# Attention, SoLU FFN and ReLU6 FFN on one core: a list scheduler gets a modelled transfer queue, a smaller cushion and another table of moves

## The chip, the cores and the metric

The kernel runs on one NeuronCore of a Trainium2 chip. The metric is the device time of one execution in microseconds (us); of several runs the median is taken.

## What is computed

Three stages in a row, all in float32 (the reference is cut to them):

```
# q, k, v: 4 x 8 heads x 576 positions x 64;  s: 4 x 8 x 576
scores = q @ k.T / sqrt(D);  cum = cumsum(max(s, 0))
scores = where(causal, -1e9, scores + min(-(cum_i - cum_j), 0))
x = softmax(scores) @ v                     # 2304 tokens x 512
h = x @ w_in                                # 512 -> 1024
solu = h * softmax(h);  x = (layernorm(solu) * g_ln) @ w_out
h = x @ w_in2                               # 512 -> 2048
g = h * clip(h + 3, 0, 6) / 6;  out = g @ w_out2
```

## The kernel before

Every float32 operand of a matmul is split into a high and a low part of reduced width, and a product is made of three matmuls (high by high, high by low, low by high). The splits are what ACT and DVE do most: ACT casts the high part, DVE subtracts it to get the low one.

**Attention** goes by pairs of heads: q and k are transposed on TensorE (L679, L639 for the first heads), stacked, the scores are made (L794, L830), the exponent is taken on ACT (L751), the rows are scaled on POOL (L846, L864), transposed (L898) and multiplied by v (L925). **The SoLU FFN** works on 18 tiles of 128 tokens: first product L1030, exponent L1047 and square L1067 on ACT, transposes L1099, second product L1120. Its tiles run in between the heads. **The ReLU6 FFN** starts when the last tile of the SoLU FFN has its second product: three groups `bi` of 768 tokens and eight slices `k` of the hidden width make 24 units. A unit does seven products of blocks on TensorE instead of eight (L1370, six matmuls each): it needs the seven forms of x (`xb`, cast at L1309 from the loaded tile `xr`), the seven forms of the weights of slice k (`ws`, cast at L480, low part at L484), and it collects its results through ACT copies out of PSUM (`c`, L1383), DVE sums (L1389), the clip on ACT (L1396) and the product on DVE (L1399). Each result `g` is stored to DRAM (`g_d`, L1404), in the last slices from POOL's queue. The second product (L1547) loads it back (`r`, L1504), splits it into forms (`fa`, `fs`, L1524) and multiplies it by the forms of the second weights (`W`, either loaded whole at L1464 or loaded into `stage` at L1453 and split at L1457 and L1460).

**What sets the order.** Nothing is issued while the program above is walked. Each operation is recorded by `plan.add(eng, us, fn, reads, writes, ...)` as one of 4138 entries with its engine, an assumed duration, and what it depends on. `Plan.emit` (L99 to L187) then plays them through: each engine takes, of the entries whose inputs are there, the one of lowest `rank`; PSUM banks and buffers are given out on the way. The entries are then issued in the order in which they started in this play, and each engine runs its own entries strictly in that order. So the assumed durations, the assumed landing times of transfers (`lag`), a cushion per engine (`plan.spare`, set at L1219 and added to every DVE and ACT entry recorded after it) and the table `MOVED` (L45), which adds a number to the rank of a range of entries, decide which instruction of an engine stands ahead of which, and nothing else. An instruction whose input is late holds up all that stand behind it on its engine.

```
for a, b, eng, places in MOVED:
    for i in range(a, b):
        if eng in (None, self.ops[i][0]):
            self.rank[i] += places
...
ready_at[j] = max(ready_at[j], end + lag + hop if done else start)
```

Of the kernel before, what the change touches and what calls it, by code (L numbers as in the profile page):

```python
# [42 lines left out]
X_RAW = 2  # L43

MOVED = (  # L45
    (2969, 3058, None, 37), (1088, 1095, None, -26), (42, 207, "ACT", -571), (89, 289, None, 22), (701, 705, None, -5000), (1603, 1616, None, -575),
    (3219, 3238, None, -136), (1310, 1376, "PE", -5000), (4000, 4010, None, 9), (3187, 3354, None, 10), (2195, 2220, None, -5000), (1728, 1743, None, 80),
    (1680, 1785, None, -19), (3311, 3318, None, 11), (1751, 1784, "DVE", 600), (3833, 3890, None, 20), (3402, 3431, None, -110), (4067, 4090, None, 5000),
    (2726, 2734, None, 7), (2064, 2078, None, 7), (3604, 3653, None, 7), (3738, 3763, None, -890), (3446, 3458, None, -1115), (193, 393, "ACT", -14),
    (99, 112, "ACT", -173),  # L50
# [4 lines left out]
class Plan:  # L55


    def __init__(self):
        self.ops, self.writers, self.users, self.rings, self.born, self.reuse = [], {}, {}, {}, {}, []
        self.takes, self.bank = {}, {}  # L60
        self.stage, self.stages = "", {}
        self.behind, self.rank, self.port = 0, [], []
        self.spare = {}

    def add(self, eng, us, fn, reads=(), writes=(), new=(), lag=0.0, bank=None, after=(), stages=(), port=None):
# [3 lines left out]
        self.port.append(eng == "POOL" if port is None else port)  # L69
        self.rank.append(op + self.behind)  # L70
# [34 lines left out]
    def emit(self):  # L105
# [30 lines left out]
        order, port_free = [], 0.0  # L136
        while len(order) < n:
# [25 lines left out]
            us, lag = self.ops[i][1], self.ops[i][4]  # L163
# [3 lines left out]
            free[e] = end = start + us  # L167
            order.append((start, i))
# [15 lines left out]
        for _, i in sorted(order):  # L184
            self.ops[i][2]()

# [22 lines left out]
def kernel(ctx, tc, q, k, v, s, w_in, w_out, g_ln, w2_in, w2_out, out):  # L209
# [81 lines left out]
    def gate_rows():  # L291
# [37 lines left out]
        for i in range(len(blocks)):  # L329
            plan.add("ACT" if i >= 2 else "SP", 0.45, lambda i=i: load(i), writes=[f"s/{i}"], lag=2.0)  # L330
# [9 lines left out]
        def to_dram():  # L340
            plan.add("POOL", 0.6, lambda: nc.gpsimd.tensor_scalar(neg, first_t["cum"][: 2 * NH].bitcast(F32), -1.0, 1.0, ALU.mult, ALU.mult), reads=["gate/h", "gate/l1"], writes=["neg"])
            for x in range(2):
                r = blocks[x]
                for i, row, src, keys in ((0, 2 * x, lambda r: one[:NH], ["one"]), (1, 2 * x + 1, lambda r: one[:NH], ["one"]), (1, 2 * x, lambda r: first_t["cum"][r].bitcast(F32), ["gate/h", "gate/l1"]), (0, 2 * x + 1, lambda r: neg[r], ["neg"])):
                    plan.add("SP", 0.45, lambda i=i, row=row, src=src, r=r: put(i, row, src(r)), reads=keys, writes=[f"rows/{i}{row}"], lag=4.0)
# [13 lines left out]
    def split64(plan, pool, src, hi, lo, name, key, scale=None, bufs=1, ring="", raws64=2, after=(), hi_dve=False, on_dve=(), on_act=(), behind=None, needs=(), home=()):  # L359
# [44 lines left out]
        def put_lo():  # L404
# [3 lines left out]
            else:  # L408
# [5 lines left out]
                             lag=2.0 if behind is None else 4.0, after=after),  # L414
# [1247 lines left out]
```

## Time and profile before

| | |
|---|---|
| runs shown | 793.2, 796.46, 796.31 us; median 796.31 |
| the profiled execution | 792.05 us, span 790.3 us |
| busy: PE, DVE, ACT, POOL | 769.4 (97%), 598.3 (76%), 476.5 (60%), 233.0 us (29%) |
| mean granted TensorE clock | 0.994 |

Times in the trace are microseconds from the start of the span. The profiled execution took 1.75 us more than its span and 4.26 us less than the median of the runs. "PEclk" is the granted share of TensorE's full clock. A matmul is pipelined, so its own duration in the trace is longer than the distance to the next one; a stretch in which matmuls follow each other without a hole counts as fully busy.

### The profile page before, as it was taken

What the parts mean: (1) busy time and instruction counts of PE and PEld (TensorE: products, weight loads), DVE (VectorE), ACT (ScalarE), POOL (GpSimd) and SP (SyncE); (2) the same over time, 40 slices, a digit from 0 to 9 for tenths busy, and PEclk for the clock granted to TensorE, in tenths of its full rate; (3) what the DMA queues carried; (4) which work ended last, traced back from release to release, by engine and by line L of the source; (5) the groups of instructions that cost most, each with busy time, mean ns of one, the idle gap of its engine ahead of it and who ended that gap; (6) DMA issues with size and microseconds to landing.
All of it is one profiled execution on the core that took longest, in us unless ns stands there. A gap on an engine that the chain in (4) does not pass through costs nothing.

```text
span 790.3 us, 15882 instructions
## 1 busy us (share of the span) xinstructions
PE 769.4 (97%) x5560; PEld 706.1 (89%) x5560; DVE 598.3 (76%) x1381; ACT 476.5 (60%) x1071; POOL 233.0 (29%) x320
## 2 busy tenths in 40 slices
PE   6899999999999999999999999999998999999998
PEld 5667888988889888888999999999998999999998
DVE  5889988688967786838797898889886866666662
ACT  5979887667666666736474665666674444444341
POOL 3676726263533454243110000000131012213122
PEclk9999999999999999999999999999998999999999
DMA  9947688785587757523533544666589644444440
GB/s 208 230 144 186 167 206 219 208 211 162 135 216 181 218 138 187 142 74 114 171 97 108 188 157 177 218 213 216 178 299 377 194 146 127 127 137 130 134 134 28
DMA packets 157616, 136.34 MB, mean 173 GB/s; under 512 B 67616, under 2 KB 135200, under 8 KB 157536
## 3 DMA queue, kind: packets, MB, share of 16 engines
q1 hardware_dynamic: 153600, 122.07, 53.8%
q10 hardware_dynamic: 2400, 8.54, 3.3%
q0 software_dynamic: 1536, 4.72, 1.5%
q8 instruction: 44, 0.72, 0.4%
q14 instruction: 36, 0.29, 0.1%
HBM read 74.67 MB, written 39.39 MB: 144 GB/s over the span
## 4 chain that ended last, share of the span: by engine, by line
PE 84%; DVE 7%; DMA 6%; issue 1%; ACT 1%; POOL 1%; SPq 0%; DVEq 0%; ACTq 0%; POOLq 0%
PE bank L1547 23%; PE bank L1370 17%; PE bank L1030 11%; PE bank L1120 10%; PE bank L925 6%; PE bank L898 6%; PE bank L830 5%; PE bank L794 2%; PE bank L1099 2%; DMA stage<-wt_d 2%; DMA rawi<-in_moe_w_in_dram 2%; PE bank L679 1%; DMA xr<-x_d 1%; DMA r<-g_d 1%; DVE xb L1312 1%
## 5 line engine op out<-in xcount | busy, mean ns | idle before, releaser
L1370 PE MATMUL bank<-xb,ws 128*128 128x384 f32 x1008 | 179.4, 339 | 5.9 <-ACT c L1383 4.7
L1370 PEld LDWEIGHTS bank<-xb,ws 128*128 128x128 f32 x1008 | 177.0, 189 | 7.3 <-ACT c L1383 5.7
L1547 PE MATMUL bank<-W,fs 128*128 128x256 f32 x864 | 105.7, 282 | 0.0
L1547 PEld LDWEIGHTS bank<-W,fs 128*128 128x128 f32 x864 | 104.1, 190 | 0.0
L846 POOL TENSOR_SCALAR y<-y,rsum 128x128 f32<-128x128 f32 (+4 forms) x120 | 73.0, 627 | 91.7 <-DVE rsum L842 56.5
L751 ACT ACTIVATE y<-y,nmax 96x576 f32<-96x576 f32 (+4 forms) x140 | 83.2, 596 | 12.2 <-DVE nmax L739 7.2
L739 DVE CUSTOM_DVE_ANT_0 y<-bank,mask 96x288 f32<-96x288 f32 (+4 forms) x168 | 73.9, 465 | 20.9 <-PE bank L830 16.9
L1120 PE MATMUL bank<-zh,w_out_h 128*128 128x256 f32 x288 | 82.9, 288 | 0.0
L1547 PE MATMUL bank<-W,fa 128*128 128x256 f32 x648 | 81.1, 284 | 0.0
L1120 PE MATMUL bank<-zh,w_out_l 128*128 128x256 f32 x288 | 81.0, 281 | 0.0
L1120 PE MATMUL bank<-zl,w_out_h 128*128 128x256 f32 x288 | 80.9, 281 | 0.0
L1547 PEld LDWEIGHTS bank<-W,fa 128*128 128x128 f32 x648 | 79.5, 192 | 0.0
L1404 POOL DMA_DIRECT2D g_d<-g x24 | 13.2, 552 | 195.5 <-DVE g L1399 195.4
L1030 PE MATMUL bank<-w_in_h,xh 128*128 128x512 f32 x144 | 61.1, 424 | 2.0 <-DVE nmax L739 2.0
L1030 PE MATMUL bank<-w_in_h,xl 128*128 128x512 f32 x144 | 56.9, 395 | 0.0
L830 PE MATMUL bank<-stack 128*96 128x288 f32 (+4 forms) x288 | 56.7, 317 | 0.1
L1030 PE MATMUL bank<-w_in_l,xh 128*128 128x512 f32 x144 | 56.7, 394 | 0.0
L1120 PEld LDWEIGHTS bank<-zh,w_out_h 128*128 128x128 f32 x288 | 54.2, 188 | 1.9 <-issue 0.7
L1383 ACT COPY c<-bank 128x384 f32<-128x384 f32 x72 | 34.1, 479 | 34.6 <-PE bank L1370 32.8
L1120 PEld LDWEIGHTS bank<-zh,w_out_l 128*128 128x128 f32 x288 | 54.3, 188 | 0.4
L1120 PEld LDWEIGHTS bank<-zl,w_out_h 128*128 128x128 f32 x288 | 54.2, 188 | 0.0
L898 PE MATMUL bank<-ident,y 128*128 128x128 f32 (+2 forms) x420 | 51.8, 259 | 0.5 <-POOL y L864 0.3
(275 smaller groups left out, 1572.7 us busy)
## 6 DMA issues: line engine op xcount, KB each, us to landing
r<-g_d SPq DMA_DIRECT2D x36, 512.0 KB
g_d<-g SPq DMA_DIRECT2D x72, 192.0 KB
rawo<-in_moe_w_out_dram SPq DMA_DIRECT2D x16, 512.0 KB
rawi<-in_moe_w_in_dram SPq DMA_DIRECT2D x16, 512.0 KB
x_d<-x2s SPq DMA_DIRECT2D x36, 128.0 KB
xr<-x_d SPq DMA_DIRECT2D x6, 768.0 KB
g_d<-g POOLq DMA_DIRECT2D x24, 192.0 KB, 4.8
W<-wp_d SPq DMA_DIRECT2D x6, 768.0 KB
```

Source lines behind the costliest of these rows:

```text
L739: nc.vector.tensor_tensor_reduce(out=ys[h, t][:n, c0:c1], in0=bank(key)[:n, : c1 - c0], in1=mask[:n, 480 + n - w + c0 : 480 + n - w + c1], ...
L751: nc.scalar.activation(out=y[:n], in_=y[:n], func=AF.Exp, bias=nmax[:n, h, t : t + 1], scale=-1.0, accum_out=sums[:n, h, t : t + 1])
L794: nc.tensor.matmul(bank(keys[j])[:n, : c1 - c0], lhsT=a, rhs=b, start=(m == 0), stop=(m == 3))
L830: nc.tensor.matmul(bank(key)[:n, : c1 - c0], lhsT=ss[:, 2 - 2 * m, ST[t] : w], rhs=ss[:, 3 - 2 * m, c0:c1], start=(m == 0), stop=(m == 1))
L846: nc.gpsimd.tensor_scalar(ys[h, t][:n], ys[h, t][:n], rsum[:n, h, t : t + 1], 1.0, ALU.mult, ALU.mult)
L898: nc.tensor.transpose(bank(key)[: SZ[jj], c : c + SZ[t]], ys[h, t][: SZ[t], ST[jj] : ST[jj] + SZ[jj]], ident[: SZ[t], : SZ[t]])
L925: nc.tensor.matmul(bank(key)[j * D : (j + 1) * D, lo - c0 : c1 - c0], lhsT=vs[v_key(p, a)][:n, jj, j, :], rhs=pts[pt_key(2 * p + j, a)][:n ...
L1030: nc.tensor.matmul(bank(key), lhsT=xs[i][m // 2][:, kk, :], rhs=(w_in_l if m == 1 else w_in_h)[:, kk, f * 512 : (f + 1) * 512], start=(kk ...
L1120: nc.tensor.matmul(bank(key)[:, : 2 * P], lhsT=w_out_at(w, kk)[:, m * P : (m + 1) * P], rhs=z[:, kk, :], start=(kk == 0 and i == 0), stop= ...
L1370: nc.tensor.matmul(bank(key)[:, :W], lhsT=T[f"ws{k}"][:, WS_OF[op], a, kc * P : (kc + 1) * P], rhs=x_form(bi, op)[:, b, kc, :], start=(fir ...
L1383: nc.scalar.copy(T[to], bank(key)[:, :W])
L1547: nc.tensor.matmul(bank(b_key)[:, : 2 * P], lhsT=T[name][:, y, k, :], rhs=T[f"W{i}_{q}"][:, k - k0, w, :], start=first and k == 0 and y == ...
```

## The change

Three edits, all in the planning; the operations, their engines, their dependencies and the number of instructions of each engine stay as they are.

1. A transfer no longer lands a fixed `lag` after its issue. It is given a size (`dma=moved(rows, size)`), and all transfers pass through one queue, one after the other.
2. The cushion for DVE and ACT goes from 0.03 and 0.05 us to 0.01 and 0.02 us.
3. The 25 ranges of `MOVED` are replaced by 26 others.

```diff
+DMA_START, DMA_END = 1.3, 0.3

 MOVED = (
-    (2969, 3058, None, 37), (1088, 1095, None, -26), (42, 207, "ACT", -571), (89, 289, None, 22), (701, 705, None, -5000), (1603, 1616, None, -575),
...
+    (2125, 2234, None, 171), (3467, 3487, "DVE", -24), (1445, 1447, None, 136), (4113, 4128, None, -127), (1025, 1031, None, -31), (2338, 2339, None, -64),
...
+            if self.dma[i]:
+                dma_free = max(end + DMA_START, dma_free) + self.dma[i]
+                landed = dma_free + DMA_END - end
...
-                ready_at[j] = max(ready_at[j], end + lag + hop if done else start)
+                ready_at[j] = max(ready_at[j], end + landed + hop if done else start)
...
+def moved(rows, size):
+    return rows * (0.0087 + 0.0000368 * size) * 1.13 / 16
...
-            plan.spare = {"DVE": 0.03, "ACT": 0.05, "POOL": 0}
+            plan.spare = {"DVE": 0.01, "ACT": 0.02, "POOL": 0}
...
-                    "SP", 0.0016 * 2 * P * (k1 - k0), load, reads=[f"wt{k}/{WT_PART[i]}" for k in range(k0, k1)], writes=[f"{key}s", *first], new=ring, after=["stage"], lag=2.5),
+                    "SP", 0.0016 * 2 * P * (k1 - k0), load, reads=[f"wt{k}/{WT_PART[i]}" for k in range(k0, k1)], writes=[f"{key}s", *first], new=ring, after=["stage"], dma=moved(128, 1024 * (k1 - k0))),
...
```

All other `lag=` become `dma=` in the same way. Below line 330 the lines of the changed kernel are 9 higher.

What it does to the order: every engine's instructions are the same, 316 of 1486 PE entries, 178 of 1057 on DVE, 99 of 874 on ACT, 12 of 447 on SP and 3 of 274 on POOL stand more than five places from where they stood. Three places:

ACT, end of the first product of the ReLU6 FFN, before (`c_7` is a result of slice 7 copied out of PSUM, `g_6_01` a clipped result of slice 6, `W_2_7317` the high part of a piece of the second weights, cast out of the loaded `stage`):

```order
761 L1383 COPY c_6_7271<-bank_102 128x384
762 L1396 ACTIVATE g_6_11_7290<-c_6_7271 128x384
763 L1396 ACTIVATE g_6_10_7294<-bank_102 128x384
764 L1383 COPY c_7_7304<-bank_97 128x384
765 L1457 CAST W_2_7317<-stage 128x2x256
766 L1383 COPY c_7_7325<-bank_97 128x384
767 L1396 ACTIVATE g_6_01_7328<-c_6_7244 128x384
768 L1396 ACTIVATE g_7_00_7338<-c_7_7259 128x384
769 L1396 ACTIVATE g_7_11_7342<-c_7_7325 128x384
```

and now:

```order
763 L1392 COPY c_6_7275<-bank_96 128x384
764 L1405 ACTIVATE g_6_11_7288<-c_6_7275 128x384
765 L1405 ACTIVATE g_6_10_7297<-bank_96 128x384
766 L1405 ACTIVATE g_6_01_7309<-c_6_7242 128x384
767 L1405 ACTIVATE g_7_00_7319<-c_7_7264 128x384
768 L1392 COPY c_7_7322<-bank_101 128x384
769 L1392 COPY c_7_7347<-bank_101 128x384
770 L1466 CAST W_2_7349<-stage 128x2x256
771 L1405 ACTIVATE g_7_11_7365<-c_7_7347 128x384
```

The cast out of `stage` stood ahead of the last `c_7` copy and stands behind it now; two clips, `g_6_01` and `g_7_00`, have come ahead of both copies.

PE at the same place, before (L1370 is the first product of the FFN, L1547 the second):

```order
2517 L1370 MATMUL bank_97<-xb_5_5683,ws_6903 128x384 x6
2518 L1370 MATMUL bank_100<-xb_4_5663,ws_6903 128x384 x6
2519 L1370 MATMUL bank_97<-xb_3_5758,ws_6903 128x384 x6
2520 L1370 MATMUL bank_100<-xb_6_5643,ws_6903 128x384 x6
2521 L1547 MATMUL bank_101<-W_0_6948,fa_0_0_7164 128x256 x6
2522 L1547 MATMUL bank_101<-W_1_6981,fa_0_0_7164 128x256 x6
2523 L1547 MATMUL bank_101<-W_2_7089,fa_0_0_7164 128x256 x4
```

and now:

```order
2517 L1379 MATMUL bank_97<-xb_4_5683,ws_6888 128x384 x6
2518 L1556 MATMUL bank_98<-W_0_6967,fa_0_0_7121 128x256 x6
2519 L1379 MATMUL bank_101<-xb_5_5695,ws_6888 128x384 x6
2520 L1556 MATMUL bank_98<-W_1_6982,fa_0_0_7121 128x256 x6
2521 L1556 MATMUL bank_98<-W_2_7062,fa_0_0_7121 128x256 x4
2522 L1379 MATMUL bank_101<-xb_3_5745,ws_6888 128x384 x6
2523 L1379 MATMUL bank_97<-xb_6_5666,ws_6888 128x384 x6
```

Sixteen matmuls of the second product have come in between the last four groups of the first.

ACT some 35 us into the ReLU6 FFN, where x of the second group of tokens is split, before (`xb_6` is cast out of `xr_1`, the second of its two loaded halves; `c_0` and `c_1` are results of the first and second slice copied out of PSUM):

```order
561 L1396 ACTIVATE g_1_10_5620<-bank_102 128x384
562 L1309 CAST xb_0_5630<-xr_0_5589 128x768
563 L1396 ACTIVATE g_1_01_5640<-c_1_5546 128x384
564 L1309 CAST xb_6_5643<-xr_1_5600 128x768
565 L1396 ACTIVATE g_0_00_5652<-c_0_5591 128x384
566 L1383 COPY c_0_5654<-bank_95 128x384
567 L1309 CAST xb_4_5663<-xr_0_5589 128x768
568 L1309 CAST xb_1_5666<-xr_1_5600 128x768
569 L1383 COPY c_1_5674<-bank_99 128x384
```

and now:

```order
562 L1405 ACTIVATE g_1_10_5620<-bank_96 128x384
563 L1405 ACTIVATE g_1_01_5632<-c_1_5547 128x384
564 L1405 ACTIVATE g_0_00_5640<-c_0_5590 128x384
565 L1318 CAST xb_0_5643<-xr_0_5599 128x768
566 L1392 COPY c_0_5653<-bank_102 128x384
567 L1392 COPY c_1_5657<-bank_99 128x384
568 L1318 CAST xb_6_5666<-xr_1_5608 128x768
569 L1318 CAST xb_1_5675<-xr_1_5608 128x768
```

The cast of `xb_6` stood ahead of `g_0_00` and the copies `c_0` and `c_1` and stands behind all three now.

Four more moves are spoken of below. On ACT, at the start of the ReLU6 FFN, the casts of the first slice's weights (`ws`, L480) stood behind the two exponents of the last SoLU tile and stand ahead of them now; on DVE their low parts (L484) stand four places earlier, ahead of that tile's own steps (L1051 to L1062). On PE the products of the first group with the last slice of weights stand three to four places earlier. On ACT the cast of the first form of the second product (`fa_0_0`, L1524, out of the loaded `r`) stands four places earlier, now ahead of a `c_7` copy that PE waits for, and SP issues that load two places earlier. In the attention stage, 20 to 48 us, PE has the scores of a later block (13 places earlier) and six transposes ahead of the first matmuls of the SoLU FFN (L1030), on DVE some steps of the row maximum (L739) come 16 to 24 places earlier, and on POOL six scalings of rows (L864) stand ahead of the low part of the first SoLU tile (`xl`, L1016).

## Rows read from the trace of the kernel before

**Rows 1.** The page: busy us (share of the span) and instructions of each engine.

```profile
PE 769.4 (97%) x5560; PEld 706.1 (89%) x5560; DVE 598.3 (76%) x1381; ACT 476.5 (60%) x1071; POOL 233.0 (29%) x320
```

**Rows 2.** Waits of PE: awaited line, us in total, times, longest.

```profile
PE bank L639 <- DMA rawq<-in_q_dram: 6.0, 2, 5.4
PE bank L1370 <- ACT c L1383: 4.7, 2, 3.2
PE bank L1030 <- DVE nmax L739: 2.0, 1, 2.0
PE bank L1370 <- DVE ws L484: 1.0, 1, 1.0
```

**Rows 3.** Windows: length, busy us by engine, PEclk, DMA share, GB/s.

```profile
20.00:40.00 20.00, 17.57 (x148) 12.47 (x150) 16.12 (x65) 18.39 (x53) 12.53 (x17) 1.00 0.92 227
40.00:60.00 20.00, 18.04 (x130) 12.93 (x127) 16.37 (x46) 16.02 (x38) 16.51 (x18) 0.91 0.51 150
44.40:47.90 3.50, 3.50 (x13) 2.11 (x12) 2.69 (x8) 2.67 (x7) 3.50 (x5) 0.51 0.50 162
...
100.00:380.00 280.00, 279.87 (x2078) 241.64 (x2077) 212.48 (x651) 185.44 (x484) 119.44 (x187) 1.00 0.64 170
...
400.00:420.00 20.00, 18.85 (x147) 18.39 (x146) 18.30 (x37) 15.63 (x32) 1.52 (x3) 1.00 0.26 80
460.00:580.00 120.00, 120.00 (x690) 120.00 (x689) 102.83 (x206) 76.97 (x162) 4.11 (x8) 1.00 0.58 197
580.00:600.00 20.00, 18.60 (x106) 17.96 (x104) 13.70 (x25) 10.71 (x21) 6.40 (x12) 1.00 1.01 369
600.80:607.70 6.90, 5.88 (x21) 5.88 (x22) 4.75 (x8) 4.24 (x8) 2.15 (x4) 0.51 0.97 365
620.00:780.00 160.00, 160.00 (x1346) 160.00 (x1345) 104.60 (x97) 65.16 (x88) 34.96 (x14) 1.00 0.42 124
```

**Rows 4.** Timeline around 402 us: start, us, engine, line, operation.

```profile
401.99 0.61 ACT L480 CAST ws<-ai 128x512 fp32r<-128x512 f32 x1
...
402.65 0.44 PE L1370 MATMUL bank<-xb,ws 128*128 128x384 f32 x1
...
403.36 1.02 DVE L484 TENSOR_TENSOR ws<-ai,ws 128x512 fp32r<-128x512 f32 x2
...
404.10 0.44 PE L1370 MATMUL bank<-xb,ws 128*128 128x384 f32 x1 [1.00 <-DVE ws L484]
```

**Rows 5.** Timeline around 445 us.

```profile
444.77 0.83 ACT L1309 CAST xb<-xr 128x768 fp32r<-128x768 f32 x1 [2.08 <-DMA xr<-x_d]
...
445.50 0.52 ACT L1396 ACTIVATE g<-c 128x384 f32<-128x384 f32 x1
...
445.93 0.46 ACT L1383 COPY c<-bank 128x384 f32<-128x384 f32 x1
...
446.44 0.44 PE L1370 MATMUL bank<-xb,ws 128*128 128x384 f32 x1 [1.56 <-ACT c L1383]
```

**Rows 6.** Timeline around 601 us.

```profile
600.77 0.62 ACT L1457 CAST W<-stage 128x512 fp32r<-128x512 f32 x1 [4.55 <-DMA stage<-wt_d]
601.30 0.47 ACT L1383 COPY c<-bank 128x384 f32<-128x384 f32 x1
...
601.82 0.69 PE L1370 MATMUL bank<-xb,ws 128*128 128x384 f32 x1 [3.19 <-ACT c L1383]
```

**Rows 7.** Timeline around 584 us, ACT, and DVE before it.

```profile
568.11 0.68 DVE L484 TENSOR_TENSOR ws<-ai,ws 128x512 fp32r<-128x512 f32 x1
...
584.01 1.05 ACT L1524 CAST fa<-r 128x1024 fp32r<-128x1024 f32 x1 [1.86 <-DMA r<-g_d]
```

**Rows 8.** Chain of waits, two links: start, us from issue to landing.

```profile
577.20 6.79 DMA r<-g_d
...
591.34 9.40 DMA stage<-wt_d
```

**Rows 9.** Transfers issued from 589 to 592.4 us: number, KB, median us to landing.

```profile
g_d<-g POOLq DMA_DIRECT2D x3, 192.0 KB, 6.5
```

More of the change, by code (lines that the diff above doesn't have):

```diff
@@ L329, in gate_rows @@
         for i in range(len(blocks)):
-            plan.add("ACT" if i >= 2 else "SP", 0.45, lambda i=i: load(i), writes=[f"s/{i}"], lag=2.0)
+            plan.add("ACT" if i >= 2 else "SP", 0.45, lambda i=i: load(i), writes=[f"s/{i}"], dma=moved(32, 2304))
         plan.add("DVE", 0.55, lambda: nc.vector.memset(one, 1.0), writes=["one"])
@@ L592, in load_qk @@
                 new, room = ([("x", 2, "x0")], []) if name == "q" else ([], ["x0/raw"])
-            plan.add("SP", 1.1, lambda name=name, src=src: rows(name, src), reads=room, writes=[key], new=new, lag=4.0)
+            plan.add("SP", 1.1, lambda name=name, src=src: rows(name, src), reads=room, writes=[key], new=new, dma=2 * moved(576, 256))
     def v_key(p, a):
@@ L611, in load_v @@
         for j in range(2):
-            plan.add("SP", 0.5 + 0.5 * a, lambda j=j: values(j), writes=[f"{key}/{j}"], new=[("V", 2, key)] if j == 0 else [], lag=3.0, after=[begun(p)])
+            plan.add("SP", 0.5 + 0.5 * a, lambda j=j: values(j), writes=[f"{key}/{j}"], new=[("V", 2, key)] if j == 0 else [], dma=moved(576 if a else 256, 256), after=[begun(p)])
     def first_home(p, name):
@@ L1208 @@
     to_dram()
-    plan.add("SP", 0.5, lambda: nc.sync.dma_start(out=g_sb, in_=g_ln.rearrange("(c p) -> p c", p=P)), writes=["g"], lag=2.0, after=["HL0k/h0"])
+    plan.add("SP", 0.5, lambda: nc.sync.dma_start(out=g_sb, in_=g_ln.rearrange("(c p) -> p c", p=P)), writes=["g"], dma=moved(1024, 4), after=["HL0k/h0"])
     for b, share in enumerate(SHARES):
@@ L1468, in weights @@
                 r.append(lambda both=both, key=key, k0=k0, k1=k1, number=number: plan.add(
-                    "SP", 0.0032 * 2 * P * (k1 - k0), both, reads=[f"wt{k}/{WT_PART[i]}" for k in range(k0, k1)], writes=[f"{key}/h", f"{key}/l"], new=[(f"rm{number}", 1, key)], lag=2.5))
+                    "SP", 0.0032 * 2 * P * (k1 - k0), both, reads=[f"wt{k}/{WT_PART[i]}" for k in range(k0, k1)], writes=[f"{key}/h", f"{key}/l"], new=[(f"rm{number}", 1, key)], dma=moved(128, 2048 * (k1 - k0))))
                 continue
@@ L1504, in go @@
                 nc.sync.dma_start(out=T[key(x)], in_=g_d[bi, h, o, :, :, t * P : (t + 1) * P])
-            return lambda: plan.add("SP", 1.6, go, reads=[f"gd{bi}_{h}{o}/{k}" for k in range(NK)] + (["forms"] if mine[x] == 4 else []), writes=[key(x)], new=raw_new(x), lag=3.5)
+            return lambda: plan.add("SP", 1.6, go, reads=[f"gd{bi}_{h}{o}/{k}" for k in range(NK)] + (["forms"] if mine[x] == 4 else []), writes=[key(x)], new=raw_new(x), dma=moved(1024, 512))
         def total(to, a, b, op):
```

36 lines of the change are left out of this document (17 added, 19 removed), and 3 rows, old and new, of the table MOVED.

## The prediction

> **What bounds the kernel now.** I read the busy times first: PE is busy 769.4 us, 97% of the span [rows 1]. The number of matmuls stays, so the change can only win, or lose, what PE loses in waits and in half clock. Of the 790.3 us of the span 20.9 are not PE's (790.3 - 769.4). The waits of PE name most of them [rows 2]: 6.0 us for the first q, before any of the moves acts; 4.7 for ACT's copies of L1383, in two waits; 2.0 at L1030; 1.0 for a weight form at L484. The rest is shorter waits, the start and the last stores.
>
> Then the windows [rows 3], to place these waits and the clock. From 100 to 380 us PE is busy for 279.87 of 280 us, and from 460 to 580 and 620 to 780 all the time: there the change can win nothing. What can be won lies in 20 to 60 us (2.43 and 1.96 us not busy), 400 to 420 (1.15), around 445 and 580 to 608. In two stretches the granted clock is half, 1.2 GHz instead of 2.4: 44.4 to 47.9 (mean 0.51), after PE stood 2.0 us for L1030 [rows 2], and 600.8 to 607.7 (0.51), after it stood 3.19 us [rows 6]. Work that takes 3.5 us at this level takes 1.8 at the other, 6.9 takes 3.5. The waits of 1.00 and 1.56 us [rows 4, 5] were not followed by half clock.
>
> **The change part by part.** The new durations and landings of the play are no times of the chip; they matter only through the order that comes out. So I went through each place in which PE waits, and through the moved entries for places in which it might.
>
> *Start of the ReLU6 FFN (402 us).* PE's first L1370 matmul starts at 402.65, the next at 404.10, for one low part of the weights that DVE gives from 403.36 on, because ACT's cast ran from 401.99 to 402.60, behind two exponents [rows 4]. Back to back they would be 0.17 us apart (unit of six 1.04 us), so 1.3 us are lost here, and 0.3 before the first. In the new order ACT's cast stands ahead of both exponents and DVE's low part ahead of the tile's steps. I let it end near 402.6 and leave 0.2 us: **-1.4**. What gets later are the exponents of the last SoLU tile; its tokens are needed by the third group only, some tens of us later, which hides them.
>
> *xb_6 (445 us).* ACT's cast at 444.77 waited 2.08 us for the loaded half of x; behind it stood a clip and the copy c_0 (445.93), and for this copy PE stood 1.56 us [rows 5]. Now the clip and the copy stand ahead of the cast. They wait for PE alone, so the copy ends over 1 us before PE comes (its distance in the new order): **-1.6**, bounds 0 and -1.7. Late next is xb_6 itself: PE needs it some units of 1.04 us later, and later copies arrive within 0.2 to 0.4 us of their need, which I count below.
>
> *The end of the first product (598 to 608 us).* The cast out of stage started at 600.77 after 4.55 us of waiting, the last c_7 copy at 601.30, PE at 601.82 after 3.19 us [rows 6]. The load behind it took 9.40 us from issue to landing [rows 8]; the play assumed 2.5. Now the copy stands ahead of the cast, and PE has sixteen matmuls of the second product (0.72, 0.72 and 0.48 us) between the last first products. PE's 3.19 us go, and with them, if no other hole of this size opens, the half clock (3.4 us): 6.6. Against it: the two clips that now stand ahead of both copies need buffers freed by stores, which land late here (6.5 us from issue [rows 9]), 0.5 us; the forms of the second product are made only when the last first product is done, and PE is there with less in hand, 0.5 us. **-5.5**, bounds -6.6 and -1 (the hole only gets shorter and the clock falls all the same). The cast of stage is needed first some 4 us after this place, and is there.
>
> *Products with the last slice, three to four places earlier (566 us).* DVE gives the low part of their weights at 568.11 to 568.79 [rows 7]; the products come about 3.5 us sooner, DVE's entry only about 2. **+1.2**, bounds 0 and +2; such a wait was not followed by half clock at 1.56.
>
> *fa_0_0 ahead of a c_7 copy (580 us).* ACT starts this cast at 584.01, as soon as its load lands, after 1.86 us of waiting [rows 7]; the load was issued at 577.20 and took 6.79 us [rows 8]. On SP it now stands two places earlier, and the last result that it loads is stored about 3 us sooner. It then lands near 580.5, and the copy behind it still comes before PE needs it (582.5): 0, bounds 0 and +6.9 (below).
>
> *20 to 60 us.* 4.4 us of holes and 1.7 of half clock. The 2.0 us in front of L1030 is filled by scores and six transposes that now stand there; POOL's six scalings come ahead of xl and make L1030 itself later, and DVE's steps of the row maximum (about 1 us) push the low parts of the next heads, so two short waits grow. DVE, ACT and POOL are each busy 12 to 18 of 20 us here. **-1.5**, bounds +1 (a new hole of 1 us, clock unchanged) and -4.
>
> *All other moves and the smaller cushion.* I found about ten places at which an entry of PE now comes within 0.3 us of its input; each may cost 0 to 0.3: **+1.3** in sum, bounds 0 and +3. On SP only 12 and on POOL 3 entries move over five places; their transfers shift with PE.
>
> Sum: -1.4 - 1.6 - 5.5 - 1.5 + 1.2 + 1.3 = -7.5 us. The profiled execution, 792.05 us (span 790.3 and 1.75 around it), would take 784.5. It stands 4.26 under the median of the runs shown (796.31); carried over to it: 788.8 us. No trace shows what the runs at 796 had in addition; if it hangs on the holes removed here, the gain is larger.
>
> **A rule against it.** The new play lets all transfers through one queue in their order of issue. The trace of the stretch where it matters most does not: the load issued at 591.34 took 9.40 us [rows 8], while three stores of 192 KB that POOL issued between 589 and 592.4 took a median of 6.5 [rows 9]; at least the ones issued after 591.34 were done before it. The Trainium skill, "DMA: Bandwidth & Descriptors", section "Queues, rings and completion order", says that a DMA engine goes round the queues that have work, packet by packet, and that completion is not in order of issue. By that rule the play has SP's loads too early wherever POOL stores, as here; the trace agrees.
>
> **The rivals.** *The load of fa_0_0 comes late.* If SP's load lands as before, at 584.0, since POOL's stores are served beside it, ACT stands at its cast with a c_7 copy behind, which ends near 586 instead of before 582.5. PE then has a hole of 3.5 us, as long as the one of 3.19 that was followed by half clock: 3.5 + 3.4 = 6.9 us back, -0.6 in sum, 795.7. For it: the 6.79 us of this load, and the full DMA engines (share 1.01 [rows 3]). Against it: issue and store come earlier. It decides from 1.5 us of lateness on. Chance 0.14.
>
> *The hole at 598 us moves and the clock still falls.* Clips wait for buffers, copies stand behind them, and two holes of 1 to 2 us follow each other: of 6.6 us only 1 to 1.5 stays won, -7.5 + 4.5 = -3, 793.3. For it: a hole of 2.0 us was followed by half clock at 44.4 [rows 2, 3]. Against: the sixteen matmuls in between. Chance 0.10. That the change does nothing at all can be told from the order to be untrue.
>
> *The small cushion costs PE time in the full windows (slower).* With less slack a planned start meets inputs that are late on the chip, and 316 PE entries stand elsewhere. If each of the some 14 windows from 100 to 380 us lost as much as that from 400 to 420 does now (1.15 us [rows 3]), that is 16 us, -7.5 + 16 = +8.5, 804.8; it decides from 0.54 us per window (7.5 / 14). For it: DVE and ACT are busy 212 and 185 of these 280 us, so a late step is not made up at once. Against: 0.01 to 0.03 us per entry is small beside durations of 0.5, and I found only some ten tight places. Chance 0.14.
>
> **How the numbers follow.** Forecast 0.62, rivals 0.14, 0.10 and 0.14. About 0.5% (4 us) is what a measurement of this kernel can tell from no change. The forecast lies beyond it, below 792.3; the first two rivals lie within it, together 0.24; the third beyond it on the other side. The range goes from 783 (all of 598 to 608 won and the early stage near its bound) to 797, which takes in the first two rivals and leaves out most of the third and the far ends of the forecast.
>
> **What would show it.** PE's wait list: no wait of over 0.5 us for L1383's copies near 445 and 601; 20.00 busy near 402; granted clock full from 580 to 620; no hole near 580. A wait of PE for the last ws7 form near 562 to 566 of about 1 us. I am wrong if the wait list shows a new hole over 2 us from 60 to 400, if ACT waits over 1.5 us for the first r with PE standing behind it, or if half clock remains near 600.

## The result, and the profile after

The changed kernel took 782.81 us (median of four runs, 781.96 to 783.54), before 794.94 (four runs, 793.2 to 796.46). The ratio is 0.9848, 95% interval 0.9819 to 0.9876: 1.5% faster. Four more executions made later, beside eleven of before, gave 782.96 us and 0.9859 (0.9844 to 0.9875). Five single executions of 808 to 2615 us, far from all others of their kernel, are left out of the medians and ratios here and below. The profiled execution of the changed kernel took 783.54 us with a span of 781.7, 8.5 us less than the one of before (792.05). The forecast of 788.8 had the direction right and 6.0 us too little gain; 782.81 lies 0.2 us under the low end of the range, 783.

The page of the changed kernel, busy times, and the slices of PE and its clock:

```profile
PE 766.9 (98%) x5560; PEld 705.5 (90%) x5560; DVE 600.4 (77%) x1381; ACT 476.8 (61%) x1071; POOL 229.0 (29%) x320
...
PE   6999999999999999999999999999999999999998
...
PEclk9999999999999999999999999999999999999999
```

The work of the other engines is as before to within 4 us [rows 1]. PE's busy time fell by 2.5 us: before, some 9.4 us of it lay in the two half-clock stretches (3.50 and 5.88 [rows 3]), and now there is one of 3.4 us. Its waits now (line numbers are 9 higher):

```profile
PE bank L648 <- DMA rawq<-in_q_dram: 5.6, 2, 5.4
PE bank L648 <- DMA rawk<-in_k_dram: 1.2, 1, 1.2
PE bank L934 <- ACT pt4a L911: 0.9, 1, 0.9
PE bank L688 <- DVE HL6q L700: 0.7, 1, 0.7
PE bank L907 <- POOL y L873: 0.7, 2, 0.5
```

The waits for ACT's copies (4.7 us), for L484 (1.0) and in front of L1030 (2.0) of [rows 2] are gone from the list. Four of the five shown lie in the first 46 us; the one in front of L688 is new and stands at 101 us. The windows that answer to [rows 3]:

```profile
20.00:40.00 20.00, 18.31 (x140) 13.30 (x140) 14.68 (x63) 17.48 (x52) 12.13 (x19) 0.91 0.82 208
40.00:60.00 20.00, 19.02 (x147) 14.01 (x148) 17.05 (x53) 16.91 (x40) 16.99 (x18) 1.00 0.70 182
...
100.00:380.00 280.00, 279.30 (x2078) 241.57 (x2076) 213.05 (x656) 184.31 (x483) 118.98 (x186) 1.00 0.65 169
...
400.00:420.00 20.00, 20.00 (x158) 20.00 (x158) 18.06 (x34) 13.37 (x28) 0.86 (x2) 1.00 0.18 56
...
440.00:460.00 20.00, 20.00 (x117) 20.00 (x116) 18.24 (x29) 13.95 (x27) 0.00 (x0) 1.00 0.46 162
460.00:580.00 120.00, 120.00 (x690) 120.00 (x689) 104.84 (x210) 79.78 (x166) 5.64 (x10) 1.00 0.62 205
...
580.00:600.00 20.00, 20.00 (x124) 20.00 (x123) 13.84 (x26) 11.22 (x23) 6.79 (x13) 1.00 1.04 379
600.00:620.00 20.00, 19.65 (x163) 19.24 (x162) 16.98 (x18) 9.48 (x13) 0.77 (x2) 1.00 0.89 316
```

The places at 402 and 445 us are full, from 580 to 620 PE lacks 0.35 us, and all of them run at the full clock. One half-clock stretch is left, of 3.4 us in the first window. The place at 598 us, ACT and PE:

```profile
596.06 0.48 ACT L1392 COPY c<-bank 128x384 f32<-128x384 f32 x1 [1.94 <-PE bank L1379]
596.43 0.63 ACT L1466 CAST W<-stage 128x512 fp32r<-128x512 f32 x1
...
595.86 1.36 PE L1556 MATMUL bank<-W,fa 128*128 128x256 f32 x10
597.06 2.26 PE L1379 MATMUL bank<-xb,ws 128*128 128x384 f32 x12
...
586.78 0.32 SPq L1462 DMA_DIRECT2D stage<-wt_d  x1
```

The copy waits for PE and for nothing else. The cast behind it, for which ACT stood 4.55 us [rows 6], does not wait at all: SP issues its load at 586.8 now, at 591.3 before [rows 8].

One measure serves all runs below: the **late stretch**, from the first matmul of the ReLU6 FFN (402.65 in [rows 4]) to the start of the last matmul, as the timeline of PE shows them. Before it is 402.65 to 786.55, 383.90 us; in the changed kernel 402.90 to 778.14, 375.24 us, 8.66 us less. In these two executions the changed kernel reaches its beginning 0.25 us later than the one of before: the whole difference between them lies in the late stretch.

Start and length are those of each kernel's profiled execution. The ratio is to before's executions taken beside that kernel, so ratios compare better than medians do.

| kernel | median us | ratio to before, 95% | start of late stretch | late stretch |
|---|---|---|---|---|
| before | 794.94 | 1 | 402.65 | 383.90 |
| changed | 782.81 | 0.9848 (0.9819 to 0.9876) | 402.90 | 375.24 |
| before again | 793.88 | 0.9998 (0.9979 to 1.0016) | 403.95 | 383.99 |
| last cast behind last copy (C) | 790.4 | 0.9954 (0.9938 to 0.997) | 405.04 | 381.06 |
| 402 and 445 us (A, B) | 789.79 | 0.995 (0.9932 to 0.9968) | 404.90 | 381.17 |
| A, B, C | 788.33 | 0.9921 (0.9901 to 0.9941) | 405.05 | 377.90 |
| A, B, C, cast further back | 789.4 | 0.9956 (0.9933 to 0.9979) | 404.11 | 378.95 |
| five moves | 790.6 | 0.9961 (0.994 to 0.9983) | 405.65 | 379.40 |
| seven moves | 786.44 | 0.9891 (0.9868 to 0.9914) | 404.55 | 376.59 |
| change's order up to 318 us | 791.87 | 0.9981 (0.9963 to 0.9998) | 400.70 | 383.93 |
| change's order from 318 us | 785.23 | 0.9906 (0.9885 to 0.9928) | 403.38 | 375.25 |
| queue, small cushion, old moves | 795.3 | 1.0017 (1.0 to 1.0035) | 412.05 | 378.67 |
| queue alone | 794.42 | 0.9998 (0.9975 to 1.0022) | 410.94 | 377.51 |
| new moves alone | 811.01 | 1.023 (1.0201 to 1.0259) | 421.58 | 384.74 |
| changed, old cushion | 789.57 | 0.9936 (0.9913 to 0.9958) | 405.39 | 377.61 |
| changed, two more moves | 781.61 | 0.9844 (0.9826 to 0.9862) | 400.03 | 376.07 |
| changed again | 782.96 | 0.9859 (0.9844 to 0.9875) | 401.98 | 375.62 |

Two columns of this table say more than the pair of profiled executions did. The late stretch hardly differs between executions of one order: 383.90, 383.99 and 383.93 us where the order from 318 us on is that of before, 375.24, 375.25 and 375.62 where it is the change's. Its start differs by up to 3 us. In the nine executions with before's order up to 318 us (before twice, the six kernels with moves made by hand, and the change's order from 318 us) it lies between 402.65 and 405.65 us, 404.55 in the middle; in the three with the change's order up to there (as it is, twice, and joined to before's) it lies at 400.70, 401.98 and 402.90. So the execution that the prediction was made from was the earliest of nine at this point, and the changed kernel's first one the latest of three.

### The profile page after: what moved, and what is told of

Same layout as the page of the kernel before. It is cut to its first block, busy times and chain, and to the rows that moved or that the text cites. A ratio compares the mean times of both kernels' runs of the same rounds, so it can differ in the third digit from the quotient of the medians.

```text
span 781.7 us, 15872 instructions
## 1 busy us (share of the span) xinstructions
PE 766.9 (98%) x5560; PEld 705.5 (90%) x5560; DVE 600.4 (77%) x1381; ACT 476.8 (61%) x1071; POOL 229.0 (29%) x320
## 4 chain that ended last, share of the span: by engine, by line
PE 91%; DVE 3%; ACT 2%; DMA 2%; issue 1%; SPq 0%; ACTq 0%; DVEq 0%
PE bank L1556 22%; PE bank L1379 22%; PE bank L1129 13%; PE bank L1039 12%; PE bank L934 6%; PE bank L839 5%; PE bank L907 5%; PE bank L1108 2%; PE bank L688 1%; PE bank L803 1%; DMA s_sb<-in_s_dram 1%; DMA raw_wi<-in_moe_w_in_dram 1%; DMA V0b<-in_v_dram 0%; ACT y L760 0%; DVE y L748 0%
## 5 line engine op out<-in xcount | busy, mean ns | idle before, releaser
L1379 PE MATMUL bank<-xb,ws 128*128 128x384 f32 x1008 | 176.6, 336 | 0.0
L855 POOL TENSOR_SCALAR y<-y,rsum 128x256 f32<-128x256 f32 (+4 forms) x120 | 72.1, 618 | 103.4 <-DVE rsum L851 65.3
L760 ACT ACTIVATE y<-y,nmax 128x384 f32<-128x384 f32 (+4 forms) x140 | 83.4, 598 | 19.9 <-DVE nmax L748 18.0
L839 PE MATMUL bank<-stack 128*96 128x288 f32 (+4 forms) x288 | 58.8, 321 | 0.0
## 6 DMA issues: line engine op xcount, KB each, us to landing
W<-wp_d SPq DMA_DIRECT2D x6, 768.0 KB, 10.5
```

Source lines behind the costliest of these rows:

```text
L760: nc.scalar.activation(out=y[:n], in_=y[:n], func=AF.Exp, bias=nmax[:n, h, t : t + 1], scale=-1.0, accum_out=sums[:n, h, t : t + 1])
L839: nc.tensor.matmul(bank(key)[:n, : c1 - c0], lhsT=ss[:, 2 - 2 * m, ST[t] : w], rhs=ss[:, 3 - 2 * m, c0:c1], start=(m == 0), stop=(m == 1))
L855: nc.gpsimd.tensor_scalar(ys[h, t][:n], ys[h, t][:n], rsum[:n, h, t : t + 1], 1.0, ALU.mult, ALU.mult)
L1379: nc.tensor.matmul(bank(key)[:, :W], lhsT=T[f"ws{k}"][:, WS_OF[op], a, kc * P : (kc + 1) * P], rhs=x_form(bi, op)[:, b, kc, :], start=(fir ...
```

## The experiments

The theory was the prediction's: three entries on ACT in the wrong order make the three late holes, a weight cast behind two exponents (402 us) and two casts that wait for a load ahead of a copy that PE waits for (445 and 598 us). To move single entries without playing the whole plan anew, some kernels take before's finished order and put entries elsewhere in it, by hand (`PUT` has pairs of an entry and the entries put behind it; the lines below give names in place of their numbers):

```diff
-        for _, i in sorted(order):
+        seq = [i for _, i in sorted(order)]
+        for at, moved_ops in PUT:
+            for i in moved_ops:
+                seq.remove(i)
+            k = seq.index(at) + 1
+            seq[k:k] = moved_ops
+        for i in seq:
             self.ops[i][2]()
```

**Before again.** No edit. 

> The kernel of before once more, unchanged, to see how its own executions differ. Its shown runs took 793.2 to 796.46 us, its profiled execution 792.05 with a mean granted clock of 0.994 (two half-clock stretches of 3.41 and 6.83 us). Theory 1 (the slower executions have a half-clock stretch more, after the hole of 1.0 us at 402 or that of 1.56 us at 445): executions near 796 show a mean clock of about 0.989 (6.83 us more at half clock, worth 3.4 us) or 0.991 (3.41 more, 1.7 us), those near 792 to 793 one of 0.994. Theory 2 (the spread has another cause, transfers for instance): the clock is 0.993 to 0.994 in all of them, whatever the time.

Its twelve executions took 791.1 to 797.71 us, median 793.88. The clock says part of why: at 0.991 they took 794.7 and 796.6, at 0.996 and 0.998 from 791.1 to 792.9; but at 0.994 anything from 791.75 to 797.71. So the clock goes with some 3 us of the spread, as theory 1 said, and not with the rest. The places of theory 1 are not borne out: the profiled execution, 793.63, had three half-clock stretches of 3.4 us, from 34.0, 44.2 and 604.0 us, and none behind the holes at 402 and 445. In 20 to 60 us these are two, where the first one had one:

```profile
20.00:40.00 20.00, 18.08 (x149) 0.91 0.85 219
40.00:60.00 20.00, 18.05 (x124) 0.91 0.52 147
```

The execution of before that the prediction was made from (792.05) is thus one of its faster ones, and the median of 796.31 that was shown with it stands above all the later ones (793.7 to 794.6).

**The last cast behind the last copy (C).** 

> Before, with one thing moved by hand after the play: the cast of the last piece out of stage on ACT, and its low part on DVE, stand behind the last c_7 copy and sum instead of ahead of them. Theory 1 (that one order makes the hole of 3.19 us at 598 and the half clock behind it): no hole over 0.5 us there, the clock full from 580 to 620, the end of the profiled execution 5.5 to 6.5 us earlier than 792.05, so 785.5 to 786.5. Rival (the hole only moves to the next thing that is late, the buffers of the clipped results or the forms of the second product): a hole of 1 to 3 us nearby with or without half clock, gain 1 to 4 us.

```diff
+PUT = [(c222_7 on ACT, [W3_2 high]), (c222_7 on DVE, [W3_2 low])]
```

The hole at 598 us is gone (20.00 of 20 busy in 580 to 600, full clock from there to the last matmul), but only 2.8 us of the late stretch with it, not 6.6. Its waits show 2.4 us for forms of the second product:

```profile
PE bank L1554 <- ACT fa L1531: 1.6, 1, 1.6
...
PE bank L1554 <- ACT fs L1531: 0.8, 1, 0.8
```

The rival was right: the hole moved on. Where the other 1.4 us went was not found.

**402 and 445 us (A and B).** 

> Before, with two things moved by hand after the play: the first cast of the first slice's weights ahead of the last tile's exponents on ACT with its low part earlier on DVE (402 us), and the cast of xb_6 behind the two copies c_0 and c_1 (445 us). Theory 1 (each hole is made by that order alone): both holes gone, PE ahead of before by 1.4 to 1.7 us after 406 and by 2.9 to 3.4 us after 460; profiled execution near 789, with the hole at 598 and its half clock still there. Theory on the spread (the slower executions of before get a half-clock stretch from one of these two holes): the executions of this kernel lie close together, within about 1 us, and the median falls by more than 3.4 us against before, 5 to 7. Rival: the median falls by 3 us, and the spread stays.

```diff
+PUT = [(second, [ws0 high]), (DVE e16, [ws0 low]), (c111_1, [xb2_6 high and low, xb2_4 high, xb2_1 high])]
```

PE is busy 20.00 of 20 us from 400 to 420 and 40.00 of 40 from 420 to 460. The late stretch is 2.7 us shorter. The median is 4.3 us under that of before in the same session (794.1), between theory and rival; one of its executions took 793.62, so the spread is not gone: it does not hang on these two holes alone.

**All three (A, B, C).** 

> Before, with all three orders moved by hand, and nothing else of the change. If the three places are the whole of the gain: profiled execution 782 to 783.5 us, median within 1 us of the changed kernel's 782.81, no spread of 3 us. If the rest of the new table (over 300 PE entries moved, other bank and queue orders) matters by itself: the median stays above the changed kernel by over 2 us; if that rest costs time (the trace shows the changed kernel 0.6 us behind before at 380 us), the median is 0.5 to 1.5 us below it.

6.0 us of the late stretch, not 8.7; median 788.33, 5.5 us above the changed kernel. So the rest of the new order matters. Where 2.1 of the missing 2.7 us are lost, the waits of PE and ACT's timeline of this kernel show (lines 7 higher than before):

```profile
PE bank L1554 <- ACT fa L1531: 1.3, 1, 1.3
...
PE bank L1554 <- ACT fs L1531: 0.8, 1, 0.8
```

```profile
601.09 0.62 ACT L1464 CAST W<-stage 128x512 fp32r<-128x512 f32 x1 [3.52 <-DMA stage<-wt_d]
601.62 1.35 ACT L1403 ACTIVATE g<-c 128x384 f32<-128x384 f32 x3
...
603.24 1.03 ACT L1531 CAST fa<-r 128x1024 fp32r<-128x1024 f32 x1
```

The same late load holds ACT once more: behind its cast stand three clips and a form of the second product, `fa12_0_0`, the second that is made (the first is the one of [rows 7]).

**The cast further back.** 

> The kernel with the three orders moved by hand, but the cast out of stage stands behind the first cast of the second product's form fa_0_0 (r12) as well, and its low part behind that form's low part. With the cast only behind the c_7 copy, ACT waited 3.5 us for the load (landed at 601.1) with three clips and that form behind it, and PE stood 1.28 and 0.81 us for forms. Theory 1 (this is where 2.7 us of the late gain were lost): both waits fall under 0.3 us together, the stretch from the first matmul of the ReLU6 FFN to the last takes 375 to 376 us like the changed kernel's 375.2, median 785 to 786.5. Rival (the sixteen matmuls of the second product between the last of the first, which this kernel lacks, are needed): waits of 1 us or more stay, 377 to 378 us, median 787 to 788.5.

```diff
+PUT = [..., (fa12_0_0 high, [W3_2 high]), (fa12_0_0 low, [W3_2 low])]   # instead of behind c222_7
```

The waits for those two forms are gone. But PE then comes to the next tile sooner than its load:

```profile
614.76 1.04 ACT L1531 CAST fa<-r 128x1024 fp32r<-128x1024 f32 x1 [3.44 <-DMA r<-g_d]
...
615.86 3.92 PE L1554 MATMUL bank<-W,fa 128*128 128x256 f32 x18 [2.81 <-ACT fa L1531]
```

and a half-clock stretch follows (window 600 to 620: PE busy 17.19, clock 0.91). The late stretch got 1.05 us longer than with A, B and C: neither theory had it. The changed kernel does something else here: its cast stands where C put it, ahead of the last clips and of `fa12_0_0`, and is in time because its load was issued at 586.8 us, not at 591.1 as with A, B and C. No kernel moves that load alone.

**Five moves.** 

> Before with five things moved by hand: the three orders, the cast out of stage behind the form fa_0_0 as in the run before, and on PE the first six matmuls of the next tile (fa_0_1) behind the rest of the first tile, 12 entries later, as in the changed kernel. In the run before, the form waits were gone, but PE then stood 2.81 us for the load of that next tile (issued 606.1, landed 614.7) with a half-clock stretch behind it. Theory 1 (each hole that is filled uncovers the next thing that was late behind it, and this was the last one): no hole over 0.5 us from 400 to 640, first matmul of the ReLU6 FFN to last in 375 to 376 us (changed kernel 375.2, this chain of moves so far 383.9, 377.9, 379.0), median 784.5 to 786. Rival (another late load follows): 377 us or more.

```diff
+PUT = [..., (last matmuls of tile 0, [first matmuls of tile 1])]
```

The rival again: 379.40 us, median 790.6. The clock stayed full in the late stretch. PE no longer waits for the form, but for a copy that stands behind the same cast:

```profile
617.98 1.04 ACT L1531 CAST fa<-r 128x1024 fp32r<-128x1024 f32 x1 [3.36 <-DMA r<-g_d]
618.93 0.38 ACT L1563 ACTIVATE c<-bank 128x256 f32<-128x256 f32 x1
...
619.36 1.69 PE L1554 MATMUL bank<-W,fa 128*128 128x256 f32 x12 [3.12 <-ACT c L1563]
```

**Seven moves.** 

> The five moves and one more pair: on ACT the cast fa_0_1 of the next tile stands behind the copy c (L1383's counterpart of the second product) that PE waits for, its low part on DVE behind the sum that reads the same bank, both as in the changed kernel. In the run before, PE stood 3.12 us for that copy, which stood behind the cast, which waited 3.36 us for its load. Theory 1 (each hole has one entry on ACT that waits for a load ahead of a copy that PE needs; this is the last one): no wait of PE over 0.5 us from 580 to 640, first matmul of the ReLU6 FFN to last in 375 to 376.5 us (five moves: 379.4; changed kernel 375.2), median 785.5 to 787. Rival (a further load is late behind it): 377.5 us or more, with the hole moved again.

```diff
+PUT = [..., (c22_0_0, [fa11_0_1 high]), (ob11_0_0, [fa11_0_1 low])]
```

With the copy ahead of the cast, as in the changed kernel, the late stretch is 376.59 us, 7.3 of the 8.7 us, and the median 786.44, as theory 1 had it. It did not have the waits quite right: two of PE for copies of the second product are left, one of them of 0.7 us:

```profile
PE bank L1554 <- ACT c L1563: 1.1, 2, 0.7
```

So most of the late gain can be had by clearing this chain, entries of ACT that wait for a load, each ahead of something that PE needs. It is a second way to it: the change moves the last casts less and issues a load earlier. What makes up the last 1.4 us was not taken apart.

**The change's order up to 318 us, and from there on.** At 2110 entries both orders have issued the same set, so they can be joined there; the order and the banks stand in the kernel as tables. 

> The change's order (and PSUM banks) for everything up to about 318 us, where both orders have the same 2110 entries behind them, and the order of before for the rest. Theory 1 (the early stage gives the 1.5 us that the sum has for it, through fewer half-clock stretches between 20 and 60 us, and the fuller order costs nothing from 60 to 318): median 1 to 2.5 us below before, 791.5 to 793; the hole at 598 as before. Rival (the early part costs, as the two profiled executions alone say, +0.6 us at 380 us): median 0 to 1 us above before. Slower rival of the prediction (small cushion): PE not busy 3 us or more between 100 and 318.

> The complement: order of before up to about 318 us, the change's order for the rest. In the changed kernel the stretch from the first matmul of the ReLU6 FFN to the last one took 375.2 us, before 383.9. Theory 1: this kernel takes 8.5 to 9 us less than before, median 785 to 786, its spread like that of before (half-clock stretches at 34 to 47 us stay). If early and late are independent, e5 and this one add up to the change's 11.3 us. Rival (the early order sets up the late one, through transfers already under way): less than 7 us.

The early half gives 1.9 us of the median (ratio 0.9981, interval 0.9963 to 0.9998), the late half 8.6 (0.9906), together 10.5; the changed kernel's own median, 782.81, is 11.0 under that of before here (793.79). The late stretch is 383.93 us in the first, as before, and 375.25 in the second, as in the changed kernel. Early and late are independent within the noise, and the early part gains 0.2 to 2.9 us; in the sum it had -1.5 and the +1.3 of the other moves, which makes -0.2, at the edge of that. The executions of the first go from 789.53 to 795.18 us, those of the second from 783.86 to 787.04: neither half alone has the changed kernel's narrow spread. In its own trace the early half shows no half-clock stretch before 598 us; how many there are differs from execution to execution.

**Queue and small cushion with the old moves.** 

> The changed kernel with the old table of moves: queue model and small cushion alone. Theory 1 (a table of moves only holds for the play it was found with; ranges laid on another play hit other neighbours): slower than before, 5 to 30 us, by new holes spread over the stages. Rival (the better landing times alone put casts behind late loads, and this is what the change is worth): faster than before by 4 us or more, the hole at 598 gone.

Neither: 795.3 us, a ratio of 1.0017. Each theory holds for some of the stages. The late stretch is 5.2 us shorter; of the waits that made the three holes one is left, of 0.5 us for a `c` copy; the longer ones are for forms and copies of the second product. The stages ahead of it take 9.4 us longer than in the first execution of before, 7.5 longer than in the middle one of nine. Its windows (it is some 9 us late, so the place of 598 us lies in the last one):

```profile
40.00:60.00 20.00, 16.48 (x101) 0.83 0.68 164
...
100.00:320.00 220.00, 217.44 (x1625) 0.99 0.74 185
...
400.00:460.00 60.00, 60.00 (x409) 1.00 0.44 145
...
580.00:600.00 20.00, 20.00 (x117) 1.00 0.92 304
600.00:620.00 20.00, 18.81 (x138) 1.00 1.01 410
```

**The queue alone.** 

> Before with the modelled queue alone: old cushion, old table of moves. With the small cushion beside it (the run before this one of that kind) the three holes were gone, the stretch from the first matmul of the ReLU6 FFN to the last took 378.7 us instead of 383.9, and the stages ahead of it took 9.4 us longer. Theory 1 (the queue fills the three holes, the early loss comes from the old table on a new play): the same here, first-to-last stretch 377 to 380 us, early stages 5 to 15 us longer, median 793 to 803. Rival (the early loss came from the small cushion): early stages within 2 us of before, median 789 to 792.

```diff
-            plan.spare = {"DVE": 0.01, "ACT": 0.02, "POOL": 0}
+            plan.spare = {"DVE": 0.03, "ACT": 0.05, "POOL": 0}
 (and the old MOVED)
```

Theory 1: late stretch 377.51, start of it 410.94, median 794.42. So the early loss comes from the queue's play together with the old table, not from the cushion. A queue without any table was not made, so what the queue alone does early is not known.

**The new moves alone.** 

> Before with the new table of moves: old landing times and old cushion. Theory 1: slower than before, 5 to 30 us, as for the queue with the old table; the hole at 598 stays since the play still has the load landed 2.5 us after its issue. Rival (the table alone carries the gain): within 3 us of the changed kernel, 780 to 786.

811.01 us, 17 above before, late stretch 384.74: theory 1. PE's waits show holes all over, those for ACT's `c` copies still among them, and two for transfers:

```profile
PE bank L1370 <- ACT c L1383: 5.3, 3, 2.8
PE bank L830 <- DMA stack<-HL11k: 2.9, 1, 2.9
PE bank L830 <- DMA wt_d<-ao: 2.8, 1, 2.8
PE bank L898 <- POOL y L864: 2.3, 1, 2.3
```

**The old cushion.** 

> The changed kernel with the old cushion (0.03 and 0.05 us). Theory 1 (a table of moves holds only for the play it was found with, and the cushion is part of that play): 2 to 15 us slower than the changed kernel, 785 to 798, with small holes spread over the early stages; the places at 402, 445 and 598 stay full, since it is the queue that orders them. Rival (the size of the cushion is nearly irrelevant): within 1.5 us of 782.81.

789.57 us, some 6.7 above the changed kernel, as theory 1 had it. No place at 402 to 460 or 580 to 600 is open (60.00 of 60 and 20.00 of 20); what was lost stands elsewhere, 3.2 us for POOL's scalings in the attention stage first of all:

```profile
PE bank L907 <- POOL y L855: 3.6, 2, 3.2
PE bank L1556 <- ACT fs L1533: 1.6, 3, 0.8
PE bank L839 <- DMA stack<-HL11k: 1.6, 1, 1.6
```

A cushion changed by 0.02 to 0.03 us per entry makes another order; that says nothing of whether a small or a large one is better.

**Two more moves.** 

> The changed kernel with two moves at 31 to 35 us: on POOL the low part of a piece of the first weights behind four scalings of rows instead of ahead of them, on ACT a shift and a mask of the next piece (one waits 0.35 us for its load) behind the copies pt4a and pt5a. In the changed kernel PE stood 0.48 us for those scalings and 0.91 us for pt4a. Theory 1: both holes gone, PE 0.8 to 1.4 us ahead at 60 us, and without them fewer half-clock stretches; median 780.5 to 782. Rival (what is put back is needed next: the weights' low part comes later and L1030 with it): within 0.5 us of 782.8, or above.

```diff
+PUT = [(y5_1 scaled, [w_in_l 2 on POOL]), (pt5a, [a_wi 3, t_wi 3 on ACT])]
```

The hole for pt4a went from 0.91 to 0.18 us, the one of 0.48 for the four scalings is gone (one of 0.25 us for the next scalings came in its place), and this profiled execution had no half-clock stretch before its end:

```profile
32.95 0.65 PE L941 MATMUL bank<-pt4a,V2a 128*64 128x256 f32 x2 [0.18 <-ACT pt4a L918]
```

Another execution of it has a mean clock of 0.993, so it is not free of such stretches. It reached the FFN at 400.03 instead of 402.90 and 401.98. The median, 781.61, is 1.2 to 1.35 us under the changed kernel's two medians, but its ratio to before, 0.9844 (0.9826 to 0.9862), is not told apart from 0.9848 and 0.9859.

**The changed kernel again.** 

> The changed kernel once more, for the size of its gain against more executions of before on the same chip, and as the neighbour of the version with two more moves (781.61). If the changed kernel's executions lack the spread of before because they have one half-clock stretch at most: all within 2 us, mean clock 0.996 to 1.0, median 782 to 783.5, ratio to before 0.983 to 0.987.

As expected: 782.5 to 783.29 us, clock 0.998 to 1.0. Before, in the same session, took 791.06 to 796.3.

## What of the prediction held, and the step that failed

*The step that failed: from the profiled execution to the median.* The sum against the profiled execution gave 784.5, and the changed kernel's profiled execution took 783.54. I then carried over that the profiled execution of before stood 4.26 us under the median shown, and so came to 788.8 and to a range that begins at 783. Of the 6.0 us between 788.8 and 782.81 this step makes 4.3, the sum 1.0, and 0.7 is that the changed kernel's profiled execution stands above its median and not under it. The runs show why there was nothing to carry over. Before's executions, in all the comparisons, go from 791.06 to 798.45 us, with mean clocks from 0.989 to 0.998, and 792.05 with its start of the late stretch at 402.65, the earliest of nine, was a quick one; the changed kernel's eight go from 781.96 to 783.54, with 0.998 to 1.0. Five later sets of before had medians of 793.7 to 794.6: of the 4.26 us about 2 were this execution's luck and about 2 that of the three runs shown. The prediction had said that the gain is larger if the difference hangs on the holes removed, and then did not let the range take it in. Nor do the two reasons given for its low end reach 783: they take 1.1 and 2.5 us off 788.8, which is 785.2.

*402 and 445 us.* Forecast -1.4 and -1.6, together -3.0. Both holes are gone (400 to 420: 20.00 us busy, before 18.85), and moved alone they gave 2.7 us of the late stretch. Right.

*End of the first product.* Forecast -5.5. Of the 8.66 us of the late stretch 2.7 belong to the two places above, which leaves 5.9. Right in size. From 580 to 620 PE is busy for 39.65 us, where it was for 18.60 [rows 3] and

```profile
600.00:620.00 20.00, 18.18 (x124) 18.18 (x125) 15.34 (x19) 10.68 (x16) 2.69 (x5) 0.83 0.99 350
```

and none of it is at half clock. The reason given for it was about half of it: the cast behind the copy gave 2.8 us alone and 3.3 beside A and B, and then forms of the second product were late by 2.4 and 2.1 us, for which I had put 0.5. In the changed kernel they are late by 0.4. The rest came from other entries of the new order. Two of them are shown by the hand-made kernels (the next tile's form and its first matmuls further back, which paid only together); the earlier load of stage and the sixteen matmuls between the last of the first product, on which I had counted, were not moved alone. So here the number was better than its reason.

*566 us, +1.2.* Wrong, it did not come. PE is busy all the time from 460 to 580. I had put DVE's low part about 2 us earlier, which left it late; it stands 6.7 us earlier, at 561.40 instead of 568.11 [rows 7]:

```profile
561.40 0.68 DVE L493 TENSOR_TENSOR ws<-ai,ws 128x512 fp32r<-128x512 f32 x1
```

*fa_0_0.* Forecast 0, and so it was. Its load was issued at 570.45, 6.75 us earlier than before [rows 8], and ACT waited 0.70 us for it, with the copy behind it still in time:

```profile
575.73 1.05 ACT L1533 CAST fa<-r 128x1024 fp32r<-128x1024 f32 x1 [0.70 <-DMA r<-g_d]
```

The first rival therefore fell. What spoke for it, that SP's load of [rows 8] took 9.40 us while POOL's stores beside it took 6.5 [rows 9], stays as measured; the play with one queue was close enough to put these entries right.

*20 to 60 us.* Forecast -1.5. In the pair of profiled executions PE stood still 1.7 us less there, with 3.4 us at half clock in both. The wait of 2.0 us in front of L1030 stands in all nine executions with before's early order and in none of the three with the change's. Right.

*Other moves and the cushion, +1.3.* Right in size, and by such small waits as were forecast. From 60 to 400 us the changed kernel's waits add up to 1.6 us, and three of them, 0.7, 0.4 and 0.3 us, come back at the same places in its second execution; the first execution of before has none there, the other eight with its early order 0.2 to 1.2. The third rival, holes of over 0.54 us in each of fourteen windows, fell.

These two terms cancel in the pair, and with 0.4 us more of waiting before 20 us it reaches 402 us 0.25 us later. So the sum missed the profiled execution by 1 us and the term at 566 us alone is 1.2 of it. Over many executions the stages ahead of 402 us did gain: 1.9 us of the median with the early half alone, and 2.6 us in the start of the late stretch, from the middle one of nine (404.55) to that of three (401.98). Half-clock stretches are part of it, 3.4 to 10.2 us per execution with before's early order, 0 to 3.4 with the change's. This is the gain that the step to the median, which kept a difference of 4.26 us on both sides, left out.

*The second rival*, a hole that moves while the clock still falls, did not happen in the changed kernel. The hole moved in four of the kernels made by hand (C, A with B and C, the cast further back, five moves); the clock fell behind it in one of them, the third.

## What to carry to other kernels

Where an engine runs its entries strictly in order, an entry that waits for a transfer should not stand ahead of one that another engine needs. Look for the awaited copy, and then for the next such entry behind it: here three of the holes that were filled uncovered another. These tables of moves were worth something only on the plan that they were found with: the new table on the old plan cost 17 us, the old one on the new plan lost more ahead of the late stretch than the new plan won in it. And an execution's distance from the median of its kernel is no constant to be carried over to another kernel, least of all one with fewer holes.

## What was not expected of the hardware

A hole's length alone did not tell whether the clock falls. After 2.81 us (kernel with the cast further back) the granted clock was 0.91 in the window, with 3.4 us at half; after 3.12 us (five moves), in the same stage, it stayed full. With A and B alone it stayed full after a hole of 2.42 us, at 600.3, and fell at 620.3, behind one of 1.87 us. The windows of the first two:

```profile
600.00:620.00 20.00, 17.19 (x132) 0.91 0.98 360
```

```profile
600.00:620.00 20.00, 16.53 (x133) 1.00 1.02 386
```

In the attention stage the nine profiled executions with one and the same order (before's) had one or two half-clock stretches between 33 and 49 us, 3.4 to 10.2 us long together. What the rest of before's spread is, beside the clock, was not found: at one mean clock (0.994) its executions still differ by 6 us.
